# Projection matmuls of 64 rows issued two PSUM tiles at a time in a fused attention and GEGLU kernel

## The chip, the cores and the metric

The kernel runs on one core of one Trainium2 chip. The metric is the device time of one execution in microseconds (us). The engines are named as in the profile: PE (matrix multiplication), PEld (loading of PE's weights), DVE (vector engine), ACT (activations), POOL, and SP (which issues most DMAs here, 118 of the 152 in before). In this kernel PE writes its results to a memory called PSUM, where ACT and DVE read them.

One of the first three executions of the kernel before took 388.07 us, against 376.65 and 376.63 for the other two; at 3% above them it counts as slow and takes no part in any ratio.

## The reference, cut to what matters

Two stages follow one another: linear attention with random features, and a gated feed-forward block on its output.

```python
# q, k, v: (8 batches, 8 heads, 576, 64); omega: (128, 64); x: 4608 tokens of 512; d_ff = 1536
def phi(x):                                   # for q and k, each scaled by 64**-0.25
    h = x @ omega.T - sum(x*x)/2
    return exp(h - max(h)) / sqrt(128)
kv  = einsum('bhsm,bhsd->bhmd', k_p, v)
z   = k_p.sum(axis=2)
x   = einsum('bhsm,bhmd->bhsd', q_p, kv) / (q_p . z + 1e-6)     # then heads side by side
out = (gelu(x @ w_gate) * (x @ w_val)) @ w_out
```

The projections `x @ omega.T` contract over only 64 numbers. They are the matmuls of 64 rows that the change is about.

## The kernel before

The attention of a batch works with heads in pairs: one 128-partition tile holds two heads, and the two matmuls for `a = 0` and `a = 1` take their weights and their input from its two halves of 64 partitions. In the trace the two start 3 to 4 ns apart. The results go to PSUM tiles called pk (for k) and pq (for q). A tile's readers are the instructions that take it out of PSUM: the exp on ACT, and for pk also the maximum (nmax) on DVE.

```python
att = ctx.enter_context(tc.tile_pool(name="att", bufs=2, space=bass.MemoryType.PSUM))  # 2 tiles
mo  = ctx.enter_context(tc.tile_pool(name="mo",  bufs=4, space=bass.MemoryType.PSUM))  # 4 tiles
...
def attention(b):
    ...
    on_dma = b > 1                    # batches 2 to 7: k and q are transposed by DMA, not on PE
    ...
    for i0, n in CHUNKS:              # 5 tiles: n = 4, 4, 4, 4, 2
        pk = att_tile([P, 2, 4, M], F32, "pk")
        for i in range(n):
            for a in range(2):
                sl = slice(a * D, (a + 1) * D)
                nc.tensor.matmul(pk[:, a, i, :], kT[sl, i0 + i, :], omegaT2[sl])
        nc.scalar.activation(k_p[:, :, i0:i0 + n, :], pk[:, :, :n, :], func=Exp)
        nc.vector.reduce_max(nmax[:, :, i0:i0 + n], pk[:, :, :n, :], axis=AX, negate=True)
    ...
    for i0, n in CHUNKS:              # again 5 tiles
        pq = att_tile([P, 2, 4, P], F32, "pq")
        for a in range(2):
            sl = slice(a * D, (a + 1) * D)
            nc.tensor.matmul(pq[:, a, :n, :], omegaT2[sl], qT[sl, i0:i0 + n, :])
        for a in range(2):
            nc.scalar.activation(q_pTv[:, a, i0:i0 + n], ..., func=Exp)
        if i0 == 0:
            nc.scalar.activation(wk, nmax, func=Exp)
    ...                               # v_ext = v * wk (DVE); kz: 72 matmuls of 64 rows; copy of kz (DVE)
    ...                               # numerators nd, 5 groups of 8 matmuls; 1/den and x_sb (DVE)

# the order in which the program is written; the framework's scheduler then orders every
# engine but ACT by its own estimate of when things are ready
for t in range(N_TOK):                # 9 chunks of 512 tokens
    ...
    if t + 1 < B:
        attention(t + 1)
    if t > 0:
        project_out(t - 1)            # o_ps: 48 full matmuls
    gate_val(t)                       # g_ps, v_ps: 96 full matmuls, gelu on ACT, product on DVE
```

A "full matmul" below is one of 128 rows, 128x512: o_ps, g_ps and v_ps. There are 48 + 96 of them for each 512 tokens. They need nothing from the attention of the next batch, so the scheduler puts them between the projections, where PE would otherwise wait for ACT and DVE to empty the two `att` buffers.

The softmax here doesn't subtract the row's maximum and nothing guards it: scores larger than these inputs give would overflow.

Of the kernel before, what the change touches and what calls it, by code (L numbers as in the profile page):

```python
# [15 lines left out]
def kernel(  # L16
# [11 lines left out]
    nc = tc.nc  # L28
# [26 lines left out]
    Exp = mybir.ActivationFunctionType.Exp  # L55
    Gelu = mybir.ActivationFunctionType.Gelu
    AX = mybir.AxisListType.X
# [8 lines left out]
    def att_tile(shape, dtype, name):  # L66
        return att.tile(shape, dtype, name=name, tag="att")

    def mo_tile(shape, dtype, name):
        return mo.tile(shape, dtype, name=name, tag="mo")  # L70
# [55 lines left out]
    omegaT2 = singles.tile([2 * D, M], BF16)  # L126
# [7 lines left out]
    def put_x(c0, n, copy):  # L134
        done = 0
        while done < n:
            t, c = divmod(c0 + done, T_TOK)
            m = min(n - done, T_TOK - c)
            if t not in x_tiles:
                x_tiles[t] = work.tile([P, N_DM, T_TOK], BF16, name="xT", bufs=3)  # L140
            copy(x_tiles[t][:, :, c:c + m], done, m)
            done += m


    def transposed(nm, b, on_dma):
        src = loaded.pop((nm, b))
        t_sb = work.tile([P, NI, P], BF16, name=f"{nm}T", tag="kqT")
        if on_dma:
            nc.sync.dma_start_transpose(out=t_sb, in_=src.rearrange("p i x -> p (i x)"))
            return t_sb  # L150
        n = NI // 3
        for i0 in range(0, NI, n):
            t_ps = mo_tile([P, n, P], BF16, f"{nm}T_ps")
            for i in range(n):
                nc.tensor.transpose(t_ps[:, i, :], src[:, i0 + i, :], ident)  # L155
            nc.vector.tensor_copy(t_sb[:, i0:i0 + n], t_ps)  # L156
        return t_sb

    def attention(b):


        first = b == 0

        def two_banks(name):

            if first:
                halves = [mo_tile([P, 512], F32, name) for _ in range(2)]
                return halves, [(slice(g, g + 1), t.unsqueeze(1)) for g, t in enumerate(halves)]
            t = att_tile([P, 2, 512], F32, name)
            return [t[:, 0], t[:, 1]], [(slice(0, 2), t)]  # L170

        on_dma = b > 1
        kT = transposed("k", b, on_dma)
        qT = transposed("q", b, on_dma) if on_dma else None


        k_p = work.tile([P, 2, NI, M], BF16, name="k_p")
        nmax = work.tile([P, 2, NI], F32, name="nmax")
        wk = work.tile([P, 2, NI], F32, name="wk")
        for i0, n in CHUNKS:  # L180
            pk = att_tile([P, 2, 4, M], F32, "pk")
            for i in range(n):
                for a in range(2):
                    sl = slice(a * D, (a + 1) * D)
                    nc.tensor.matmul(pk[:, a, i, :], kT[sl, i0 + i, :], omegaT2[sl])  # L185
            nc.scalar.activation(k_p[:, :, i0:i0 + n, :], pk[:, :, :n, :], func=Exp)  # L186
            nc.vector.reduce_max(nmax[:, :, i0:i0 + n], pk[:, :, :n, :], axis=AX, negate=True)  # L187


        if not on_dma:  # L190
            qT = transposed("q", b, False)
        q_pT = work.tile([P, 2, NU, SP], BF16, name="q_pT")
        q_pTv = q_pT.rearrange("m e (i a) p -> m a i e p", a=2)
        for i0, n in CHUNKS:
            pq = att_tile([P, 2, 4, P], F32, "pq")
            for a in range(2):
                sl = slice(a * D, (a + 1) * D)
                nc.tensor.matmul(pq[:, a, :n, :], omegaT2[sl], qT[sl, i0:i0 + n, :])  # L198
            for a in range(2):
                nc.scalar.activation(q_pTv[:, a, i0:i0 + n],  # L200
                                     pq[:, a, :n, :].rearrange("m i (e p) -> m i e p", e=2),
                                     func=Exp)
            if i0 == 0:
                nc.scalar.activation(wk, nmax, func=Exp)  # L204


        vf = loaded.pop(("v", b))
        ve = work.tile([P, NU, DP1], BF16, name="v_ext")
        vev = ve.rearrange("p (i a) c -> p i a c", a=2)
        wkv = wk.rearrange("p a i -> p i a")  # L210
        vfv = vf.rearrange("p j y -> p (j y)").rearrange("p (i a d) -> p i a d", a=2, d=D)
        for half in range(2):
            isl = slice(half * NI // 2, (half + 1) * NI // 2)
            nc.vector.tensor_mul(vev[:, isl, :, :D], vfv[:, isl],  # L214
                                 wkv[:, isl].unsqueeze(3).broadcast_to((P, NI // 2, 2, D)))
            nc.vector.tensor_copy(vev[:, isl, :, D], wkv[:, isl])


        kz_ps, kz_groups = two_banks("kz_ps")
        for j in range(HP):  # L220
            for r in range(R):
                u = R * j + r
                for e in range(2):
                    sl = slice(e * SP, (e + 1) * SP)
                    nc.tensor.matmul(kz_ps[e][:, j * DP1:(j + 1) * DP1],  # L225
                                     k_p[sl, u % 2, u // 2, :], ve[sl, u, :],
                                     start=(r == 0), stop=(r == R - 1))
        kz = work.tile([P, 2, HP * DP1], BF16, name="kz")
        for gs, t in kz_groups:
            nc.vector.tensor_copy(kz[:, gs], t[:, :, :HP * DP1])  # L230

        def numerators(r0):
            nr = min(2, R - r0)
            n = nr * SP
            nd, groups = two_banks("nd")
            for h in range(H):
                j, e = divmod(h, 2)
                u = R * j + r0
                nc.tensor.matmul(nd[h // 4][:n, (h % 4) * DP1:(h % 4 + 1) * DP1],  # L239
                                 q_pT[:, e, u:u + nr, :].rearrange("m r p -> m (r p)"),  # L240
                                 kz[:, e, j * DP1:(j + 1) * DP1])
            x_sb = work.tile([P, d_model], BF16, name="x_sb", bufs=10)
            iden = work.tile([P, 2, 4, 1], F32, name="iden", bufs=4)
            for gs, t in groups:
                ndv = t[:n, :, :4 * DP1].rearrange("p g (h c) -> p g h c", c=DP1)
                nc.vector.reciprocal(iden[:n, gs], ndv[:, :, :, D:DP1])
                nc.vector.tensor_mul(  # L247
                    x_sb[:n].rearrange("p (g h d) -> p g h d", g=2, h=4)[:, gs],
                    ndv[:, :, :, :D],
                    iden[:n, gs].broadcast_to((n, gs.stop - gs.start, 4, D)))  # L250
            return r0, n, x_sb

        def place(r0, n, x_sb):
            c0 = b * S + r0 * SP
            if on_dma:
                put_x(c0, n, lambda dst, o, m: nc.sync.dma_start_transpose(
                    out=dst, in_=x_sb[o:o + m, :]))
                return
            xt_ps = (mo_tile if first else att_tile)([P, N_DM, P], BF16, "xt_ps")
            for c in range(N_DM):  # L260
                nc.tensor.transpose(xt_ps[:, c, :n], x_sb[:n, c * P:(c + 1) * P],  # L261
                                    ident[:n, :n])
            put_x(c0, n, lambda dst, o, m: nc.vector.tensor_copy(dst, xt_ps[:, :, o:o + m]))

        ahead = None
        for r0 in range(0, R, 2):
            block = numerators(r0)
            if ahead is not None:
                place(*ahead)
            ahead = block  # L270
        place(*ahead)
# [42 lines left out]
    with tc.manual_schedule(engines={mybir.EngineType.Activation}):  # L314
        attention(0)
        for t in range(N_TOK):
            if t + 2 < B:
                load_kq("k", t + 2)
                load_kq("q", t + 2)
                load_v(t + 2)  # L320
# [3 lines that stand above are left out]
                project_out(t - 1)  # L324
            gate_val(t)
        project_out(N_TOK - 1)
# [30 lines left out]
```

## Time and profile before

| | before |
|---|---|
| median of the first three executions | 376.65 us (376.63 to 388.07) |
| profiled span | 374.4 us |
| PE, DVE, ACT busy | 94%, 56%, 42% |
| PE's share of the chain that ended last | 88% |
| length of one period (batches 2 to 7) | 37.98 us |

From the page of the kernel before, busy time of each engine with its share of the span, and the chain of work that ended last:

```profile
PE 352.7 (94%) x2673; PEld 167.2 (45%) x2673; DVE 208.8 (56%) x341; ACT 156.5 (42%) x250; POOL 26.0 (7%) x40
...
PE 88%; DVE 5%; ACT 2%; DMA 2%; POOL 1%; issue 0%; POOLq 0%
```

PE is the bottleneck, and everything else matters only where it makes PE wait or makes PE do its work less efficiently.

The trace has six equal periods, one for each of the batches 2 to 7, which begin with the first pk matmul of a batch. Here is PE in the first part of one period of the kernel before (start, length in us up to the modelled end, source line, operation, how many):

```profile
144.26 0.62 PE L185 MATMUL pk<-omegaT_106,kT 64*128 64x128 bf16 x16
144.82 3.41 PE L308 MATMUL o_ps<-w_out_sb,gated 128*128 128x512 bf16 x15
148.16 0.40 PE L185 MATMUL pk<-omegaT_106,kT 64*128 64x128 bf16 x8
148.49 0.82 PE L308 MATMUL o_ps<-w_out_sb,gated 128*128 128x512 bf16 x3
149.25 0.40 PE L185 MATMUL pk<-omegaT_106,kT 64*128 64x128 bf16 x8
149.57 1.47 PE L308 MATMUL o_ps<-w_out_sb,gated 128*128 128x512 bf16 x6
150.98 0.28 PE L185 MATMUL pk<-omegaT_106,kT 64*128 64x128 bf16 x4
151.19 1.04 PE L308 MATMUL o_ps<-w_out_sb,gated 128*128 128x512 bf16 x4
152.16 0.39 PE L198 MATMUL pq<-qT,omegaT_106 64*128 64x512 bf16 x2
152.49 0.39 PE L308 MATMUL o_ps<-w_out_sb,gated 128*128 128x512 bf16 x1
...
156.88 1.33 PE L225 MATMUL kz_ps<-v_ext,k_p 64*128 64x65 bf16 x72
```

PE goes nine times to the projections (pk 16, 8, 8, 4 and five times pq 2), each time between full matmuls. The individual start times show what a visit costs. Full matmuls in a row start 216 ns apart. The last one before a visit is followed by the first 64-row matmul after 312 ns, 96 more. The two matmuls of a pair start 3 to 4 ns apart, and from the second of a pk pair to the first of the next it is 52 or 53 ns; but after the last pair the next full matmul comes only after 148 ns, again 96 more. The repeats just after each border are some 10 ns longer (63 instead of 52 or 53 ns, 226 instead of 216). I call these two places borders, and one visit a round trip; it costs about 0.21 us beyond its work. At a border the figure changes that the profile writes beside the operation, 64*128 or 128*128. I call it the tiling mode; in these traces it goes with the rows*columns of the weights (weight loads of 64x128 for pk and pq, 128x128 for the full matmuls).

In the groups by shape the weight loads show the same; columns after the bar: busy us, mean ns, idle us before them and what ended it:

```profile
L185 PEld LDWEIGHTS <-kT 64*128 64x128 bf16 x288 | 9.3, 100 | 15.5 <-issue 14.9 <-DVE kT L156 0.6
L198 PEld LDWEIGHTS <-omegaT_106 64*128 64x128 bf16 x80 | 4.7, 94 | 19.0 <-issue 13.9 <-PE pq L198 2.5 <-PE o_ps L308 2.5
```

"Issue" means that nothing the profile can name was waited for. Some 29 us of idle of the weight loader ended that way; the loads of full matmuls run ahead of their matmuls (each starts 1 or 2 ns after the matmul before it), but these do not: at a border the load starts 307 or 308 ns after the last full matmul.

### The profile page before, as it was taken

To read this page: it belongs to the slowest core of one execution; us is meant where nothing else is said; L and a number is where in the kernel's file an instruction comes from. 1 tells how busy PE (TensorE), PEld (TensorE's weight loads), DVE (VectorE), ACT (ScalarE), POOL (GpSimd) and SP (SyncE) were. 2 spreads that over 40 slices of the span, in tenths; PEclk is the share of its full clock that TensorE was granted. 3 is DMA by queue.
4 is the path that set the end of the run, shared out by engine and by line. 5 is a ranking of instruction groups with operands and counts; after the bars stand their busy time and mean duration, and the time that the engine had idled before them with its cause. 6 is when DMAs were issued, how large, how long until landed. Compare 5 with 4: busy or idle time off the path is not lost.

```text
span 374.4 us, 6513 instructions
## 1 busy us (share of the span) xinstructions
PE 352.7 (94%) x2673; PEld 167.2 (45%) x2673; DVE 208.8 (56%) x341; ACT 156.5 (42%) x250; POOL 26.0 (7%) x40
## 2 busy tenths in 40 slices
PE   4489699999999999999999999999999999999994
PEld 2356354444444444444444444444354444444441
DVE  2777784676367735864577358734864323323431
ACT  2442833654366336633673357335733203303310
POOL 8223000210001000100000000000000000000000
PEclk9999999999999999999999999999999999999999
DMA  7999999999607999799289306700242040022013
GB/s 122 267 271 206 207 269 161 243 217 245 126 2 154 115 106 182 141 143 234 41 155 202 73 2 137 157 12 0 56 73 50 0 95 19 0 59 56 0 30 86
DMA packets 64239, 44.12 MB, mean 118 GB/s; under 512 B 44752, under 2 KB 57552, under 8 KB 64208
## 3 DMA queue, kind: packets, MB, share of 16 engines
q1 hardware_dynamic: 48816, 20.10, 32.1%
q0 software_dynamic: 15392, 23.60, 31.4%
q8 instruction: 21, 0.34, 0.4%
q14 instruction: 10, 0.08, 0.1%
HBM read 37.78 MB, written 9.44 MB: 126 GB/s over the span
## 4 chain that ended last, share of the span: by engine, by line
PE 88%; DVE 5%; ACT 2%; DMA 2%; POOL 1%; issue 0%; POOLq 0%
PE o_ps L308 27%; PE g_ps L284 25%; PE v_ps L290 24%; PE pq L198 3%; PE nd L239 3%; PE kz_ps L225 3%; PE pk L185 3%; DVE nmax L187 2%; DMA q_in<-in_q_dram 2%; ACT q_pT L200 2%; DVE x_sb L247 1%; DVE qT L156 1%; PE kT_ps L155 1%; PE xt_ps L261 0%; PE qT_ps L155 0%; POOL k_in L87 0%
## 5 line engine op out<-in xcount | busy, mean ns | idle before, releaser
L292 DVE TENSOR_TENSOR gated<-g_gelu,v_ps 128x512 bf16<-128x512 bf16 x108 | 74.1, 686 | 99.1 <-PE v_ps L290 96.6
L287 ACT ACTIVATE g_gelu<-g_ps 128x512 bf16<-128x512 f32 x108 | 64.4, 597 | 131.3 <-PE g_ps L284 131.3
L284 PE MATMUL g_ps<-xT,w_gate_sb 128*128 128x512 bf16 x432 | 112.9, 380 | 0.3 <-ACT g_gelu L287 0.3
L290 PE MATMUL v_ps<-xT,w_val_sb 128*128 128x512 bf16 x432 | 111.4, 379 | 0.0
L308 PE MATMUL o_ps<-w_out_sb,gated 128*128 128x512 bf16 x432 | 105.1, 381 | 0.0
L290 PEld LDWEIGHTS <-w_val_sb 128*128 128x128 bf16 x432 | 42.1, 98 | 49.6
L284 PEld LDWEIGHTS <-w_gate_sb 128*128 128x128 bf16 x432 | 41.2, 98 | 46.7 <-issue 0.8
L308 PEld LDWEIGHTS <-gated 128*128 128x128 bf16 x432 | 37.4, 98 | 45.1 <-issue 5.4
L186 ACT ACTIVATE k_p<-pk 128x1024 bf16<-128x1024 f32 (+1 forms) x40 | 36.7, 937 | 35.5 <-PE pk L185 35.0
L187 DVE TENSOR_REDUCE nmax<-pk 128x8 f32<-128x1024 f32 (+1 forms) x40 | 42.7, 1113 | 9.6 <-ACT k_p L186 9.5
L200 ACT ACTIVATE q_pT<-pq 128x512 bf16<-128x512 f32 (+1 forms) x80 | 37.4, 586 | 5.3 <-PE pq L198 5.3
L311 DVE COPY o_sb<-o_ps 128x512 f32<-128x512 f32 x36 | 24.4, 678 | 22.6 <-PE o_ps L308 22.6
L247 DVE TENSOR_TENSOR x_sb<-nd,iden 128x512 bf16<-128x512 f32 (+3 forms) x45 | 27.8, 626 | 0.9
L214 DVE TENSOR_TENSOR v_ext<-vf,wk 128x1152 bf16<-128x1152 f32 x16 | 21.7, 1358 | 5.8 <-ACT wk L204 5.8
L287 ACT ACT_TABLE_LOAD x7 | 9.0, 1283 | 28.7 <-PE g_ps L284 28.7
L198 PE MATMUL pq<-qT,omegaT_106 64*128 64x512 bf16 (+1 forms) x80 | 15.8, 387 | 4.5 <-ACT q_pT L200 2.6
L239 PEld LDWEIGHTS <-q_pT 128*128 128x128 bf16 (+1 forms) x320 | 13.6, 104 | 10.9 <-DVE x_sb L247 4.7
L185 PE MATMUL pk<-omegaT_106,kT 64*128 64x128 bf16 x288 | 15.2, 234 | 2.8 <-DVE nmax L187 2.5
L239 PE MATMUL nd<-kz,q_pT 128*128 128x65 bf16 (+1 forms) x320 | 17.0, 201 | 0.6 <-DVE kz L230 0.5
L185 PEld LDWEIGHTS <-kT 64*128 64x128 bf16 x288 | 9.3, 100 | 15.5 <-issue 14.9
L225 PEld LDWEIGHTS <-k_p 64*128 64x128 bf16 x576 | 11.7, 103 | 3.9 <-issue 3.8
L225 PE MATMUL kz_ps<-v_ext,k_p 64*128 64x65 bf16 x576 | 12.7, 203 | 0.7 <-ACT q_pT L200 0.7
(31 smaller groups left out, 94.7 us busy)
## 6 DMA issues: line engine op xcount, KB each, us to landing
vf<-in_v_dram POOLq DMA_DIRECT2D x8, 1152.0 KB, 13.0
out_dram<-o_sb SPq DMA_DIRECT2D x72, 128.0 KB, 2.4
q_in<-in_q_dram POOLq DMA_DIRECT2D x8, 576.0 KB, 11.0
k_in<-in_k_dram POOLq DMA_DIRECT2D x7, 576.0 KB, 7.8
w_gate_sb<-in_moe_w_gate_dram POOLq DMA_DIRECT2D x3, 512.0 KB, 22.2
w_val_sb<-in_moe_w_val_dram POOLq DMA_DIRECT2D x3, 512.0 KB, 21.9
w_out_sb<-in_moe_w_out_dram POOLq DMA_DIRECT2D x3, 512.0 KB, 21.6
k_in<-in_k_dram POOLq DMA_DIRECT2D x2, 288.0 KB, 4.5
```

The lines of the kernel that those rows point to most:

```text
L185: nc.tensor.matmul(pk[:, a, i, :], kT[sl, i0 + i, :], omegaT2[sl])
L186: nc.scalar.activation(k_p[:, :, i0:i0 + n, :], pk[:, :, :n, :], func=Exp)
L187: nc.vector.reduce_max(nmax[:, :, i0:i0 + n], pk[:, :, :n, :], axis=AX, negate=True)
L200: nc.scalar.activation(q_pTv[:, a, i0:i0 + n], pq[:, a, :n, :].rearrange("m i (e p) -> m i e p", e=2), func=Exp)
L225: nc.tensor.matmul(kz_ps[e][:, j * DP1:(j + 1) * DP1], k_p[sl, u % 2, u // 2, :], ve[sl, u, :], start=(r == 0), stop=(r == R - 1))
L239: nc.tensor.matmul(nd[h // 4][:n, (h % 4) * DP1:(h % 4 + 1) * DP1], q_pT[:, e, u:u + nr, :].rearrange("m r p -> m (r p)"), kz[:, e, j * DP ...
L247: nc.vector.tensor_mul(x_sb[:n].rearrange("p (g h d) -> p g h d", g=2, h=4)[:, gs], ndv[:, :, :, :D], iden[:n, gs].broadcast_to((n, gs.sto ...
L284: nc.tensor.matmul(g_ps, w_gate_sb[:, jm, fs], xT[:, jm, :], start=(jm == 0), stop=(jm == N_DM - 1))
L287: nc.scalar.activation(g_gelu, g_ps, func=Gelu)
L290: nc.tensor.matmul(v_ps, w_val_sb[:, jm, fs], xT[:, jm, :], start=(jm == 0), stop=(jm == N_DM - 1))
L292: nc.vector.tensor_mul(gated[:, jf, :], g_gelu, v_ps)
L308: nc.tensor.matmul(o_ps, gated[:, jf, qq * P:(qq + 1) * P], w_out_sb[:, jf, :], start=(jf == 0), stop=(jf == N_DFF - 1))
```

## The change

The intent: two tiles in a row (a pair) share one visit. The first tile of a pair waits for the readers of both earlier tiles (those of one because it takes over that tile's buffer, those of the other by the added dependency), so that both buffers are free and the second can follow at once. Only batches 2 to 7 are affected.

```diff
+        readers, count = [], [0]
+
+        def paired(mm):
+            if count[0] % 2 == 0 and on_dma:
+                for ins in readers:
+                    tc.add_manual_dep(mm.ins, ins.ins.name, mybir.DependencyInfo(
+                        mybir.DependencyClass.Sync, mybir.DependencyReason.DATA))
+            count[0] += 1
+            readers.clear()
...
-                    nc.tensor.matmul(pk[:, a, i, :], kT[sl, i0 + i, :], omegaT2[sl])
-            nc.scalar.activation(k_p[:, :, i0:i0 + n, :], pk[:, :, :n, :], func=Exp)
-            nc.vector.reduce_max(nmax[:, :, i0:i0 + n], pk[:, :, :n, :], axis=AX, negate=True)
+                    mm = nc.tensor.matmul(pk[:, a, i, :], kT[sl, i0 + i, :], omegaT2[sl])
+                    if i == a == 0:
+                        paired(mm)
+            readers += [
+                nc.scalar.activation(k_p[:, :, i0:i0 + n, :], pk[:, :, :n, :], func=Exp),
+                nc.vector.reduce_max(nmax[:, :, i0:i0 + n], pk[:, :, :n, :], axis=AX,
+                                     negate=True)]
...                                   # the same for pq: paired() at a == 0, both exps are readers
```

The diff does not say where the full matmuls go. The scheduler places them, and the order of the built program shows where:

```
before: pk16 o15 pk8 o3 pk8 o6 pk4 o4 pq2 o1 pq2 o3 pq2 o2 pq2 o3 pq2 o3         kz72 o4 nd16 ...
after:  pk16 o20 pk16 o14 pk4 pq2 o6 pq4 o8 pq4 g4 v1                            kz72 v3 g1 nd16 ...
```

The fifth pk tile pairs with the first pq tile. Nine visits become five.

More of the change, by code (lines that the diff above doesn't have):

```diff
@@ L197, in attention @@
                 sl = slice(a * D, (a + 1) * D)
-                nc.tensor.matmul(pq[:, a, :n, :], omegaT2[sl], qT[sl, i0:i0 + n, :])
+                mm = nc.tensor.matmul(pq[:, a, :n, :], omegaT2[sl], qT[sl, i0:i0 + n, :])
+                if a == 0:
+                    paired(mm)
             for a in range(2):
-                nc.scalar.activation(q_pTv[:, a, i0:i0 + n],
-                                     pq[:, a, :n, :].rearrange("m i (e p) -> m i e p", e=2),
-                                     func=Exp)
+                readers.append(nc.scalar.activation(
+                    q_pTv[:, a, i0:i0 + n],
+                    pq[:, a, :n, :].rearrange("m i (e p) -> m i e p", e=2), func=Exp))
             if i0 == 0:
```

## The prediction

> **What bounds the kernel.** TensorE: the page gives PE 94% busy of a 374.4 us span and 88% of the chain of work that ended last. DVE (56%) and ACT (42%) bind only locally. The timeline shows six equal periods of 37.98 us (batches 2 to 7: attention of the next batch between output and gate matmuls); there the chain of waits is practically all PE.
>
> **What an interruption costs.** In the trace, 128x512 matmuls in a row start 216 ns apart. Before 64-row matmuls the last full one takes 312 ns (96 more); from the last pk pair to the next full matmul 148 ns pass, against 52 between pk pairs (96 more); the first repeats afterwards are some 10 ns longer on each side. A round trip costs about 0.21 us beyond the work. [...]
>
> **What the change does.** It adds no instruction and no work. In the order of the built programs the borders between 64-row and 128-row matmuls fall from 134 to 86: 24 round trips fewer, four in each period. Before, the groups are pk 16, 8, 8, 4, pq 2, 2, 2, 2, 2, kz 72; after, pk 16, 16, 4+pq 2, pq 4, pq 4, kz 72, with 20, 14, 6, 8 and 5 full matmuls between. Alone this is worth 24 x 0.21 = 5.0 us (1.3%).
>
> **What it gives back.** Each pair now waits for both earlier tiles' readers[...]. I walked one period by hand with measured durations (estimates; time from the first pk, us):
> - Second pk pair: nmax of tile 2 ends at 4.57, PE gets there at 4.98: no stall.
> - pk+pq: nmax of tile 4 ends 3.41 after its k_p began, at 8.83; PE at 8.63: stall about 0.26.
> - pq 2 and 3: exp of pq 1 ends about 10.8; PE 10.72: stall about 0.14.
> - pq 4 and 5: four exps (0.48 apart) end about 13.33; PE 13.23: stall about 0.15.
> - kz: free.
> - DVE's order after kz now has the first gated product (after an ACT table load of 1.28 and a gelu of 0.60) before the first reciprocals: the third nd group, waiting for x_sb, stalls about 0.25.
>
> These sum to 0.8 us a period against 0.84 saved, plus 0.08 that before itself lost at one pq. Nearly all of the 5 us is on the critical path, and nearly all comes back as waits: net gain about 0.15 us a period, 1 us in all.
>
> **Prediction:** 375.6 us, 372.6 to 379.0. Faster by over 2%: 0.01; within 2%: 0.97; slower: 0.02.
>
> **What would show it.** Timeline: 16 pk together; the projections' groups fall from nine to five per period. Groups by shape: idle before the pk and pq weight loads put down to "issue" (14.9 and 13.9 us) falls to roughly half, and new waits appear: pk on nmax (about 6 x 0.26), pq on q_pT (6 x 0.3), nd on x_sb (6 x 0.25). The last full matmul before a waiting pair lasts about 0.45 us instead of 0.31. A period is 37.8 us.
>
> **What would make it wrong.** If the readers end a little earlier than in my walk, the stalls vanish and up to 5 us are gained (371.5); each 0.2 us of error in each of four waits moves the result by 5 us the other way. Other risks: an output copy ahead of nmax on DVE, waiting for an output DMA; the gelu's timing moving the DVE order's stall; the slow execution seen once in before (388 us).

0.84 us saved and the 0.08 us that before lost at one pq, against 0.8 us of waits, leave 0.12 us, which it puts at about 0.15 us a period, 1 us in all. What the walk needs is in the trace of before: at the fourth pq the step from the last full matmul was 394 instead of 312 ns, and the o_ps matmuls behind it, which need nothing from pq and the first two of which only continue a sum already begun, came 320 ns after its second matmul, as at the other pq. A matmul that waited thus held up those behind it.

## The result and the profile after

| | before | after |
|---|---|---|
| first comparison: median, range | 376.89 us (4 runs, one of them slow at 388.07) | 376.69 us (376.09 to 377.28, 4 runs) |
| ratio of fast runs | | 0.9997, 95% interval 0.9975 to 1.0019 |
| profiled span, mean granted clock | 374.4 us, 0.993 | 374.9 us, 0.979 |
| length of a period | 37.98 us | 37.77 us |
| first pk of batch 2 (start of the first period) | 68.30 us | 70.11 us |

A ratio is the mean time of one kernel's fast runs over that of the other's fast runs of the same rounds, so it is not quite the ratio of the medians.

The lines of the page after that answer to those of before:

```profile
PE 349.2 (93%) x2673; PEld 166.8 (44%) x2673; DVE 207.0 (55%) x341; ACT 156.6 (42%) x250; POOL 26.0 (7%) x40
...
PE 68%; ACT 15%; DVE 11%; DMA 2%; issue 1%; POOL 1%; POOLq 0%
```

The busy shares hardly moved. The chain did: PE's share has fallen by 20 points, and those of ACT and DVE have risen by 13 and 6. PE in the same part of a period, after:

```profile
145.64 0.62 PE L197 MATMUL pk<-omegaT_106,kT 64*128 64x128 bf16 x16
146.20 4.49 PE L326 MATMUL o_ps<-w_out_sb,gated 128*128 128x512 bf16 x20
150.62 0.62 PE L197 MATMUL pk<-omegaT_106,kT 64*128 64x128 bf16 x16
151.17 3.20 PE L326 MATMUL o_ps<-w_out_sb,gated 128*128 128x512 bf16 x14
154.53 0.29 PE L197 MATMUL pk<-omegaT_106,kT 64*128 64x128 bf16 x4 [0.16 <-DVE nmax L202]
154.65 0.38 PE L214 MATMUL pq<-qT,omegaT_106 64*128 64x512 bf16 x2
154.96 1.47 PE L326 MATMUL o_ps<-w_out_sb,gated 128*128 128x512 bf16 x6
156.49 0.60 PE L214 MATMUL pq<-qT,omegaT_106 64*128 64x512 bf16 x4
157.02 1.90 PE L326 MATMUL o_ps<-w_out_sb,gated 128*128 128x512 bf16 x8
159.04 0.50 PE L214 MATMUL pq<-qT,omegaT_106 64*128 64x512 bf16 x4
```

The pairs are there. Of the waits PE's own lines show only one, 0.16 us, because the modelled end of a matmul lies long after the next one could start (a full one is given 379 ns, and the next starts after 216): at 154.53 the last o_ps had started at 153.99, some 540 ns earlier, where 312 would do. The weight loads show more:

```profile
L257 PEld LDWEIGHTS <-q_pT 128*128 128x128 bf16 x256 | 10.7, 100 | 9.5 <-DVE x_sb L265 5.9 <-DVE kz L248 1.9 <-issue 1.2
L197 PEld LDWEIGHTS <-kT 64*128 64x128 bf16 x288 | 9.3, 100 | 14.3 <-issue 7.2 <-DVE nmax L202 6.5 <-DVE kT L156 0.6
L214 PEld LDWEIGHTS <-omegaT_106 64*128 64x128 bf16 x80 | 3.3, 95 | 14.4 <-issue 7.5 <-ACT q_pT L218 6.9
```

"Issue" has halved for both projections (14.9 to 7.2, 13.9 to 7.5), and waits for nmax and for the exps have taken its place. These sums hold the ordinary 0.42 us that the loader idles before every visit too, so they are not the loss itself; that has to be read from start times.

The chain of waits after, in the same stretch, says what the waits hang on (start, us, what):

```profile
150.69 0.35 PE pk L197 x8
...
151.06 1.03 ACT k_p L201
...
152.11 0.98 DVE nmax L202
...
153.26 1.23 DVE nmax L202
...
154.53 0.30 PE pk L197 x4
...
154.86 0.60 ACT k_p L201
155.45 0.99 ACT q_pT L218 x2
...
156.49 0.41 PE pq L214 x2
...
156.92 2.08 ACT q_pT L218 x4
...
159.04 0.41 PE pq L214 x2
```

From one visit to the next the time is now that of the readers: pk, exp, two reductions, pk and pq, exp, exp, pq, four exps, pq. PE has work to fill these times, but a little too little of it was put there.

Further on PE waits once more. DVE after, from the copy of kz on:

```profile
162.03 0.70 DVE L248 CAST kz<-kz_ps 128x520 bf16<-128x520 f32 x1 [1.97 <-PE kz_ps L243]
163.05 0.69 DVE L310 TENSOR_TENSOR gated<-g_gelu,v_ps 128x512 bf16<-128x512 bf16 x1 [0.32 <-ACT g_gelu L305]
163.66 0.27 DVE L264 RECIPROCAL iden<-nd 128x8 f32<-128x8 f32 x2
163.89 1.29 DVE L265 TENSOR_TENSOR x_sb<-nd,iden 128x512 bf16<-128x512 f32 x2
```

The first gated product stands before the reciprocals, waits for its gelu, and so x_sb, whose end frees the buffer for the third nd group, is late.

The trace gives all of it as entries, the time from the start of the last full matmul to the start of the first matmul of a visit (one period of each trace; in the others the figures differ by a few ns). Among the kernels of the experiments only these columns are needed later:

| entry, ns | before | after | gated_late | fill_only | fill_late |
|---|---|---|---|---|---|
| second pk pair | (two visits, 311 and 312) | 311 | 311 | 312 | 311 |
| pk 5 (and pq 1) | 312 and 312, two visits | 540 | 539 | 320 | 323 |
| pq 2, 3 | 321 and 312, two visits | 434 | 435 | 311 | 312 |
| pq 4, 5 | 394 and 312, two visits | 495 | 493 | 492 | 312 |
| third nd group | 303 | 487 | 301 | 486 | 298 |
| **period, us** | **37.98** | **37.77** | **37.57** | **37.42** | **37.06** |

The account of a period: four round trips of 0.21 us are saved, and the 82 ns that before lost at one pq (394 against 312): 0.92 us. Given back are 540 - 312 = 0.23, 434 - 312 = 0.12, 495 - 312 = 0.18 and 487 - 303 = 0.18 us: 0.72 us before the terms are rounded. The rest is 0.20 us; the two periods differ by 0.22 us, 1.3 us in six.

That first comparison showed no gain at all. In its two profiled executions the reason is in the trace: the start of the program was 1.8 us longer with the change. Why is a question for the experiments.

### The profile page after: what moved, and what is told of

Same layout as the page of the kernel before. It is cut to its first block, busy times and chain, and to the rows that moved or that the text cites. A ratio compares the mean times of both kernels' runs of the same rounds, so it can differ in the third digit from the quotient of the medians.

```text
span 374.9 us, 6519 instructions
## 1 busy us (share of the span) xinstructions
PE 349.2 (93%) x2673; PEld 166.8 (44%) x2673; DVE 207.0 (55%) x341; ACT 156.6 (42%) x250; POOL 26.0 (7%) x40
## 4 chain that ended last, share of the span: by engine, by line
PE 68%; ACT 15%; DVE 11%; DMA 2%; issue 1%; POOL 1%; POOLq 0%
PE v_ps L308 22%; PE g_ps L302 22%; PE o_ps L326 15%; ACT q_pT L218 9%; DVE nmax L202 6%; ACT k_p L201 3%; ACT L305 2%; DMA q_in<-in_q_dram 2%; PE nd L257 2%; PE pk L197 2%; DVE x_sb L265 2%; PE pq L214 2%; ACT g_gelu L305 1%; DVE gated L310 1%; DVE qT L156 1%
## 5 line engine op out<-in xcount | busy, mean ns | idle before, releaser
L302 PE MATMUL g_ps<-xT,w_gate_sb 128*128 128x512 bf16 x432 | 114.3, 382 | 0.3 <-ACT g_gelu L305 0.3
L308 PE MATMUL v_ps<-xT,w_val_sb 128*128 128x512 bf16 x432 | 114.0, 381 | 0.0
L326 PE MATMUL o_ps<-w_out_sb,gated 128*128 128x512 bf16 x432 | 97.9, 380 | 0.0
L326 PEld LDWEIGHTS <-gated 128*128 128x128 bf16 x432 | 40.3, 98 | 50.7 <-issue 4.1
L308 PEld LDWEIGHTS <-w_val_sb 128*128 128x128 bf16 x432 | 41.3, 98 | 48.1 <-issue 0.5
L302 PEld LDWEIGHTS <-w_gate_sb 128*128 128x128 bf16 x432 | 40.3, 98 | 46.7 <-issue 2.0
L218 ACT ACTIVATE q_pT<-pq 128x512 bf16<-128x512 f32 (+1 forms) x80 | 38.1, 567 | 6.3 <-PE pq L214 6.3
L214 PE MATMUL pq<-qT,omegaT_106 64*128 64x512 bf16 (+1 forms) x80 | 13.6, 383 | 5.5 <-ACT q_pT L218 2.6
L197 PE MATMUL pk<-omegaT_106,kT 64*128 64x128 bf16 x288 | 14.2, 233 | 3.8 <-DVE nmax L202 3.4
L87 POOL DMA_DIRECT2D k_in<-in_k_dram x9 | 6.7, 749 | 94.1 <-DMA kT<-k_in 88.5
```

The costliest lines, as they stand in the source:

```text
L197: mm = nc.tensor.matmul(pk[:, a, i, :], kT[sl, i0 + i, :], omegaT2[sl])
L218: readers.append(nc.scalar.activation(q_pTv[:, a, i0:i0 + n], pq[:, a, :n, :].rearrange("m i (e p) -> m i e p", e=2), func=Exp))
L302: nc.tensor.matmul(g_ps, w_gate_sb[:, jm, fs], xT[:, jm, :], start=(jm == 0), stop=(jm == N_DM - 1))
L308: nc.tensor.matmul(v_ps, w_val_sb[:, jm, fs], xT[:, jm, :], start=(jm == 0), stop=(jm == N_DM - 1))
L326: nc.tensor.matmul(o_ps, gated[:, jf, qq * P:(qq + 1) * P], w_out_sb[:, jf, :], start=(jf == 0), stop=(jf == N_DFF - 1))
```

## The experiments

Ten runs were made, eight of them of new kernels; all gave correct results. "Before" ran beside them on the same chip each time; three chips were used. The theory: the 96 ns at each border come from the change of tiling mode; pairing saves four round trips; PE gives most of it back (0.72 of 0.92 us a period) at four places, where too few full matmuls or DVE's order make it wait. The first part was the author's guess, from the mode that changes just there, until rows128 measured it. Where the expectations below are marked as cut, they named a mechanism for it that no run shows, or the same rule for PE's order as the forecast.

### Is there a gain at all: after_again and before_again

The edit: none; the changed kernel and the kernel before once more.

> The changed kernel unaltered, to settle its small difference. Theory [...]: a period of 37.77 us against 37.98, so 1.3 us less in six periods, ratio about 0.9965; the first trace showed this gain and a start 1.8 us longer, which the theory takes for scatter of the start (input landing, granted clock), since the order of instructions there is the same. Rival (the change itself makes the start longer): periods 37.77 again, the first pk of the third batch again near 70.1 us instead of 68.3, ratio 1.000.

> The kernel before once more, for a second profile of its start. Theory (the start scatters with the landing of inputs and the granted clock): the first pk of the third batch is not again at 68.3 us but nearer to the 69.2 to 70.1 us seen in three profiles of changed kernels; periods 37.98 us. Rival (the changed kernels' start is longer by their own doing): 68.3 again, within 0.3 us.

Measured: after_again 376.19 us (375.76 to 377.95, 6 runs) against 377.90 us, ratio 0.9959, interval 0.9938 to 0.998. Its period is 37.77 us, its first period begins at 69.60 us. before_again (one run, 378.42 us, so its state is unknown) has the same 37.98 us as before, but its first period begins at 70.53 us instead of 68.30.

So the rival falls: the start of one and the same kernel differs by 2.2 us between two executions. It was rather the profiled execution of before that was unusual: its 68.30 us is the shortest start of all twelve traces, and the others lie between 68.97 and 71.63 us. Part of the scatter is the granted clock. The stretch from 31 to 69 us (busy time of PE, PEld, DVE, ACT, POOL; granted clock; DMA share; GB/s) in before:

```profile
31.00:69.00 38.00, 34.35 (x325) 18.91 (x325) 25.35 (x45) 18.35 (x30) 5.21 (x7) 0.96 1.19 204
```

and in before_again:

```profile
31.00:69.00 38.00, 33.62 (x306) 18.82 (x309) 25.25 (x47) 17.00 (x28) 5.21 (x7) 0.85 1.18 205
```

In this part of the program the clock records of before show half clock once, for 3.41 us, and those of before_again twice, for 6.83 us each. The two views cover the same time but not quite the same work, so the cost is read from batch 1's first pk to batch 2's: 35.14 us in before and 35.21 in after_again (clock 0.96 in the stretch above), 36.11 in before_again (0.85) and 36.34 in the first profile of the changed kernel (0.86). Of the 1.8 us of the first comparison 1.2 lie here. Clock is not all of it: after_again had the same 0.96 as before, and began its first period 1.3 us later. There the second half of the first k transposes began at 9.20 us instead of 7.48, after the input had landed.

A change of 1.3 us cannot be judged by single executions whose start scatters by 2 us. The period can: within one trace the periods agree to 8 ns.

### Where the 96 ns come from: rows128

The kernel before, with omega padded by zeros, so that the projections run on all 128 rows. The order of instructions on PE is the same, and so are all waits; only the tiling mode of pk and pq differs, and with it the length of a visit, since the two matmuls of a pair of pk, 3 to 4 ns apart in before, now start some 56 ns apart.

```diff
-    omegaT2 = singles.tile([2 * D, M], BF16)
+    omegaT2 = singles.tile([2 * D, 2, M], BF16)
+    nc.vector.memset(omegaT2, 0.0)
...
-                    nc.tensor.matmul(pk[:, a, i, :], kT[sl, i0 + i, :], omegaT2[sl])
+                    nc.tensor.matmul(pk[:, a, i, :], kT[:, i0 + i, :], omegaT2[:, a])
...
-                nc.tensor.matmul(pq[:, a, :n, :], omegaT2[sl], qT[sl, i0:i0 + n, :])
+                nc.tensor.matmul(pq[:, a, :n, :], omegaT2[:, a], qT[:, i0:i0 + n, :])
```

> Before, with the k and q projections on all 128 rows (omega padded with zeros), same order of instructions on PE and no pairing. Theory [...]: at the nine borders of a period around pk and pq the extra 96 ns go (full matmul to pk 216 instead of 312 ns; pk to full matmul about 56), saving 9 x 0.21 = 1.9 us, while the projections, no longer two at a time, take 1.1 us (pk) and 1.0 us (pq) more: period about 38.1 us, time about 377.5, ratio 1.002. Rival (the 96 ns come from the semaphore wait or the first weight load of a new operand): borders stay at 312 and 150 to 200 ns, period about 40.0 us, ratio about 1.03.

Measured: 380.94 us, ratio 1.0080 (1.0055 to 1.0104), period 38.41 us. PE in the timeline, where the visits are now written 128*128:

```profile
149.35 3.40 PE L307 MATMUL o_ps<-w_out_sb,gated 128*128 128x512 bf16 x15
152.59 0.61 PE L185 MATMUL pk<-omegaT,kT 128*128 128x128 bf16 x8
153.04 0.81 PE L307 MATMUL o_ps<-w_out_sb,gated 128*128 128x512 bf16 x3
```

The first three entries to pk are 215, 216 and 215 ns instead of 312, and the full matmul follows 56 ns after the last pk instead of 148. kz was left on 64 rows, and its entry is still 312 ns. So the 96 ns belong to the change of tiling mode, and not to the semaphore wait or to the first load of another operand, both of which are still there. The rival is out. The changed kernel says the same: from pk to pq, another operand in the same mode, it takes 52 or 53 ns.

A second rival, that the 96 ns are a weight load that PE has to sit through (one takes 92 to 99 ns around these borders), was not tested by a kernel, but the traces speak against it. At a border the load starts only 4 ns before its matmul. At the one pq of before that waits for its readers the load comes after 308 ns, 87 ns ahead of the matmul, and yet PE is back at the full matmuls after the same 319 ns or so as at the other pq. In rows128 the load starts 1 or 2 ns after the last full matmul, even where the matmul then waits. So the change of mode holds up load and matmul alike. What PE does in the 96 ns no run here shows.

The period was 0.3 us over the 38.1 that the theory expected. The traces show why: without the 96 ns PE arrives earlier and waits for readers instead (entries of 362, 261, 237, 237 and 451 ns where 216 would do, 0.47 us in all, against some 0.09 us in before, nearly all of it the 82 ns at one pq). Some of the 96 ns had been covering waits. The changed kernel does the same in another form. Its three waiting visits start 56 to 58 ns after the end of the reader that they waited for, and those of rows128, which change no mode, after 50 to 54 ns, so the 96 ns were not paid on top of the wait going in.

### Pairing in part: pq_only

```diff
-            if count[0] % 2 == 0 and on_dma:
+            if count[0] % 2 == 0 and count[0] > 5 and on_dma:
```

> Pairing for the pq tiles from the second on only; the pk groups stay 16, 8, 8, 4. Theory: two round trips less (0.42 us), no wait at pk, none at the second pq group (entry 312 ns), the third pq group still some 490 ns; period 37.98 - 0.42 + 0.18 - 0.08 = 37.66 us, a little better than pairing all (37.77): ratio to before about 0.994. Rival (pairing pays only when all tiles are paired): period 37.8 to 38.0.

Measured: 374.94 us against 377.73, ratio 0.9925 (0.9912 to 0.9939), period 37.56 us. The visits are pk 16, 8, 8, 4 and pq 2, 4, 4. The second pq group enters after 312 ns, the third after 492, as expected; the third nd group after 216 instead of 303 ns, which had not been expected and is most of the 0.10 us by which the period is shorter than the 37.66 expected. So pairing only part is worth more here than pairing all (37.77). The two further round trips save 0.42 us. They bring waits of 0.23 and 0.12 us at the projections, which would still leave a gain; it is the third nd group (487 instead of 216 ns, 0.27 us) that turns it into a loss, and that wait comes from DVE's order, as the next run shows.

### Undoing the wait at nd: gated_late

The changed kernel; the first gated product of a period must come behind the x_sb products in DVE's order. (The edge fixes order only, and adds no wait.)

```diff
-            nc.vector.tensor_mul(gated[:, jf, :], g_gelu, v_ps)
+            prod = nc.vector.tensor_mul(gated[:, jf, :], g_gelu, v_ps)
+            if jf == 0 and 2 <= t + 1 < B:
+                tc.add_manual_dep(prod.ins, x_muls[t + 1].ins.name, mybir.DependencyInfo(
+                    mybir.DependencyClass.NoSync, mybir.DependencyReason.DATA))
```

> The changed kernel with only DVE's order mended: the first gated product of a period comes behind the x_sb products. Theory (the third nd group waits because DVE sits in the first gated product waiting for gelu): its entry falls from 487 to about 310 ns, the three projection waits stay (540, 434, 495 ns), period 37.77 - 0.18 = 37.6 us, six periods 1.1 us less than after: ratio to before about 0.993. Rival (nd waits for the kz copy or for PSUM buffers, not for DVE's order): period stays 37.77.

Measured: 374.96 us against 377.90, ratio 0.9916 (0.9896 to 0.9936), period 37.57 us. The third nd group enters after 301 ns; the three entries of the projections are 539, 435 and 493 ns as in the changed kernel (table above). What the wait at nd cost was DVE's order.

### Filling the waits at the projections: fill_only

The changed kernel, with edges of order that put more full matmuls ahead of the pairs. To write them, `project_out` is traced before `attention`, which gets a higher priority in exchange; without the numbers in `fill_at` this gives the same order on PE as the changed kernel (by my check of the built program; no run shows it).

```diff
+    fill_at = {2: 19, 4: 35, 6: 42, 8: 48}     # tile of the batch: full matmuls that must be ahead
...
+            if on_dma and fill_at.get(count[0]) is not None:
+                tc.add_manual_dep(mm.ins, fillers[fill_at[count[0]] - 1].ins.name,
+                                  mybir.DependencyInfo(mybir.DependencyClass.NoSync, ...))
```

> The changed kernel with more full matmuls issued ahead of the pairs (20, 15, 7, 8 instead of 20, 14, 6, 8), nothing else. Theory ([...] the scheduler put too few full matmuls ahead): entries of pk+pq and of the second pq group fall from 540 and 434 to about 312 ns; the third pq group (495) and the third nd group (487) keep their waits; period 37.77 - 0.34 = 37.43 us, ratio to before about 0.991. Rival (the waits only move, because the chain pk, k_p, nmax, exp, pq, exp is itself the length of the stage): pq groups come later by what is filled in and wait longer after, period stays 37.7 to 37.8.

Measured: 374.17 us against 377.90, ratio 0.9899 (0.9882 to 0.9916), period 37.42 us (expected 37.43). Entries of the first two pairs 320 and 311 ns, of the third still 492, of nd still 486: each as expected, and the rival (the waits only move on) falls. One full matmul more ahead of each of two visits took away 0.34 us a period, with edges of order alone.

### All four at once: fill_all, a miss

To put nine full matmuls ahead of the last pq pair, four of the gate's own (g_ps of its first column block) are traced before the attention.

```diff
-    fill_at = {2: 19, 4: 35, 6: 42, 8: 48}
+    fill_at = {4: 35, 6: 42, 8: 51}
...
+            first_gate = gate(t, 0) if 0 < t < B - 1 else None      # before attention(t + 1)
```

> The changed kernel with 20, 15, 7 and 9 full matmuls ahead of its pairs, the first gate group traced early enough to serve as such, which also puts DVE's first gated product behind three x_sb reciprocals. Theory ([...] each can be filled): all four entries (pk+pq 540, pq 434 and 495, nd 487 ns) fall to 301 to 330 ns, period 37.77 - 0.23 - 0.12 - 0.18 - 0.19 = 37.05 us, time some 4.3 us under the changed kernel, ratio to before about 0.985. Rival (gains of single waits don't add up, since one wait hides behind another): period 37.2 us or more.

Measured: 381.62 us against 377.73, ratio 1.0102 (1.0088 to 1.0116), period 38.67 us: slower. The three projection entries are right (323, and 311 at the third pq group; one matmul record is missing from the trace at the second). DVE shows where the time went:

```profile
160.06 0.68 DVE L348 COPY o_sb<-o_ps 128x512 f32<-128x512 f32 x1
163.85 0.69 DVE L327 TENSOR_TENSOR gated<-g_gelu,v_ps 128x512 bf16<-128x512 bf16 x1 [3.11 <-ACT g_gelu L321]
164.46 0.69 DVE L258 CAST kz<-kz_ps 128x520 bf16<-128x520 f32 x1
```

and so does PE at the first nd group:

```profile
165.21 0.67 PE L267 MATMUL nd<-kz,q_pT 128*128 128x65 bf16 x16 [1.45 <-DVE kz L258]
```

I had checked DVE's order from the copy of kz on, and overlooked that the scheduler had moved the first gated product ahead of that copy. DVE waited 3.11 us for the gelu with the copy behind it, and the first nd group entered after 1829 ns instead of 216. The loss of 1.61 us turns the 37.05 expected into 38.66. DVE did not take the copy first while the gated product waited: the last kz matmul ended at 162.78 us by the profile, and the copy began only at 164.46, as the gated product came to its end.

### The same with the copy first: fill_late

fill_all with the edge of gated_late.

```diff
+            if jf == 0 and 2 <= t + 1 < B:
+                tc.add_manual_dep(prod.ins, x_muls[t + 1].ins.name, ...NoSync...)
```

> fill_all with one more order edge: the first gated product behind the x_sb products on DVE, as in gated_late. fill_all lost because DVE took the first gated product before the copy of kz, and the first nd group waited 1.8 us for that copy. Theory: with the copy first again, nd enters at 216 ns, the third nd group at about 300, all projection entries stay at 311 to 323: period 37.05 us, ratio to before about 0.985. Rival (an early gate tile costs by itself, by holding a PSUM buffer and delaying later gate tiles): the time lost turns up at a g or v entry instead, period above 37.3 us.

Measured: 372.38 us against 377.51, ratio 0.9852 (0.9831 to 0.9873), period 37.06 us (expected 37.05). The table above has its entries: of the four waits 11 ns are left, at pk 5. From its timeline of the weight loads, whose idle before a visit is now the ordinary one:

```profile
153.49 0.11 PEld L208 LDWEIGHTS <-kT 64*128 64x128 bf16 x4 [0.43 <-DVE nmax L213]
...
155.53 0.11 PEld L225 LDWEIGHTS <-omegaT 64*128 64x128 bf16 x4 [0.42 <-ACT wk L233]
...
158.12 0.12 PEld L225 LDWEIGHTS <-omegaT 64*128 64x128 bf16 x4 [0.42 <-ACT q_pT L229]
```

In the changed kernel these three lines read 0.65, 0.55 and 0.61 us.

The gain over the kernel before is 37.98 - 37.06 = 0.92 us a period: just the four round trips and the 82 ns of the account above. That is the whole worth of the change when nothing is given back.

### A border of another kind: fill_all_nd128 and fill_late_nd128

The last nd group of a batch has only 64 columns of weights. In these two kernels it runs 128 columns wide in batches 2 to 7; half of its output is not used.

```diff
+            p0 = SP if on_dma and nr == 1 else 0
...
-                nc.tensor.matmul(nd[h // 4][:n, ...], q_pT[:, e, u:u + nr, :]...
+                us = slice(u - p0 // SP, u + nr)
+                nc.tensor.matmul(nd[h // 4][:p0 + n, ...], q_pT[:, e, us, :]...
...                                   # and x_sb is read from partition p0 on
```

> As fill_all, and the last nd group of a batch, 64 columns wide, run 128 columns wide (half of its output unused), in batches 2 to 7. Theory [...]: its entry falls from 309 to 216 ns and the next full matmul comes 29 instead of 128 ns after it, so 0.19 us less a period: 36.86 us, 1.2 us in all, ratio to before about 0.981. Rival (that entry is a wait for x_sb on DVE, as the two nd groups before show at times): entry stays near 300 ns and only the exit improves, period 36.95 or more.

> fill_late with the last nd group 128 columns wide in batches 2 to 7. Theory: its two borders cost 0.23 us a period, as between fill_all_nd128 and fill_all (38.674 to 38.440): period 36.82 us, ratio to before about 0.981. Rival (gain hidden behind another wait once the rest is tight): the same period as fill_late.

Measured: fill_all_nd128 380.05 us against 377.73, ratio 1.0064 (1.005 to 1.0078), period 38.44 us, which is 0.23 less than fill_all; the period of 36.86 that I had written down failed with fill_all for the same reason, the copy of kz. fill_late_nd128: 370.59 us against 377.51, ratio 0.9814 (0.9793 to 0.9835), period 36.83 us, 0.23 less than fill_late. In both pairs the entry of that group fell from 309 to 215 or 216 ns, and the next full matmul comes 29 to 33 ns after it instead of 128 or 129. The rival (a wait for x_sb) falls. A change in the number of columns costs about the same as one in the number of rows: 93 ns going in and 99 coming out. The rest of the 0.23 us are the longer first repeats, 52 instead of 29 ns in the group and 226 instead of 216 ns after it. This kernel is the best that I found: 1.9% faster than before.

## Why the prediction was right

The prediction was 375.6 us, 372.6 to 379.0, with the time within 2% of before. Measured were 376.69 us in the first comparison and 376.19 us in the second. The predicted 375.6 over 376.65 is a ratio of 0.9972. It lies inside the interval of the second comparison (0.9938 to 0.998) and just outside that of the first (0.9975 to 1.0019), whose profiled execution of the changed kernel had the longer start; the periods of the traces give 1.3 us. That a whole execution came out so near is in part luck: the base of 376.65 us, like the profiled start of 68.30 us, was at the short end of what before showed later (medians of 377.5 to 377.9 us), and the scatter of the start is as large as the gain. The period of 37.8 us is not luck, since its terms came true one by one:

- "A round trip costs about 0.21 us beyond the work": shown, and so is what it goes with, the change of tiling mode. rows128 took the 96 ns away without touching PE's order or the semaphores, and fill_late gained in full what four round trips are worth.
- "24 round trips fewer, four in each period": so it was in the trace.
- The walk through one period: the second pk pair without a stall, as predicted. pk+pq 0.26 predicted, 0.23 measured; pq 2 and 3 0.14 and 0.12; pq 4 and 5 0.15 and 0.18; nd 0.25 and 0.18. Their sum, 0.8 us, was 0.72. gated_late, fill_only and fill_late took these waits away one after another, and the period fell by what each had measured.
- "Nearly all of the 5 us is on the critical path, and nearly all comes back as waits": yes. 0.92 us of saved work of PE a period became 0.72 us of waiting.
- "A period is 37.8 us": 37.77.
- The halving of "issue" before the weight loads, the new waits for nmax and q_pT: as predicted, though their sums (6.5 and 6.9 us) hold the ordinary idle before each visit as well and can't be read as the loss.
- "The last full matmul before a waiting pair lasts about 0.45 us": 0.54, 0.43 and 0.50.
- Not foreseen: that the start of the program scatters by more than the gain. In the profiled pair this hid the gain; the first comparison showed nothing (0.9997), although each period had become shorter.

What made this walk reliable was that the order of the built program was known, and that all its durations (the reach from pk to nmax, the spacing of exps, the table load) stood in the trace of before. With the diff alone one might have counted on the whole 5 us.

## What to carry to other kernels

Where small-row matmuls are mixed with full ones, count the changes of tiling mode and measure one (96 ns going in and 96 coming out here); grouping them pays in full only if enough other matmuls stand ahead of each group to cover the readers that it waits for, because here a matmul that waited held up those behind it, and a saved border became a wait at the next semaphore (0.72 of 0.92 us a period; with enough full matmuls ahead and DVE's order mended, in fill_late, 11 ns). After such a change compare the entry of each group with its ordinary length, move work ahead of those that are too long, and look again at the order of the other engines, since the scheduler may put a waiting instruction in front of the one that PE needs (3.11 us on DVE in fill_all). Judge a gain of a few tenths of a per cent by the repeating part of the trace, not by whole executions whose start scatters.
